# Seven block products in place of eight for a gelu MLP's second matrix product: block sums on GpSimd, partial sums in the output buffer

## The chip, the cores and the metric

The kernel runs on one core of one Trainium2 chip. The metric is device time in microseconds (us).

A profile is one execution. Its span is about 1.8 us shorter than the device time of the same run (323.7 against 325.46 us in the kernel before). Shares, waits and tile times below are of spans.

## The reference

A sliding-window attention, and then a two-layer MLP with gelu (tanh form) on its output.

```python
def _attn_ref(q, k, v):                      # 8 batches, 8 heads, 576 positions, 64 wide
    scores = scale * np.matmul(q, k.transpose(0, 1, 3, 2))
    scores = np.where(np.abs(pos[:, None] - pos[None, :]) <= 32, scores, -1e9)
    ...                                      # softmax
    return np.matmul(attn, v)

def _moe_ref(x, w_in, w_out):                # x 4608x512, w_in 512x2048, w_out 2048x512
    h = x @ w_in
    g = 0.5 * h * (1.0 + np.tanh(c * (h + 0.044715 * h * h * h)))
    return g @ w_out
```

The change touches only the last line, `g @ w_out`.

## The kernel before

The 4608 tokens are worked in nine tiles of 512. For each tile, the first product makes gT (2048 x 512, transposed, fp16) in 16 groups of four matmuls, each closed by a gelu on ScalarE. The second product makes the tile's output in four blocks of 128 tokens, each of 16 matmuls of 512 columns. Between those matmuls the attention of the next batch is strewn by a plan: `s` scores, `v` weighing of the values, `m` masks, `x` the spread of the result.

```python
    def ffn_in(t, fc, d0=0, d1=4):
        ...
        for dc in range(d0, d1):
            nc.tensor.matmul(ph, w_in16[:, dc, fc * 128:fc * 128 + 128],
                             xT[:, dc, t * 512 % RING:t * 512 % RING + 512],
                             start=(dc == 0), stop=(dc == 3))
        if d1 == 4:
            nc.scalar.activation(gTs[t][:, fc, :], ph, AF.Gelu_apprx_tanh)

    def ffn_out(t, t4, fc):
        ...                                  # the last block of the last tile in two halves of 256 columns
            nc.tensor.matmul(py[:, cols], gTs[t][:, f, t4 * 128:t4 * 128 + 128],
                             w_out16[:, f, cols], start=(f == 0), stop=(f == NF - 1))
        if f == NF - 1:
            yo = yp.tile([128, 512], FP32, name="yo", tag="yo")      # yp has 3 buffers
            ...                              # one copy out of PSUM, then the stores of the block
    ...
    for t in range(NT):
        ...
            if att and b > 1:
                cast_and_turn(b)             # VectorE casts of q and k, DMA transposes
            for fc in range(begun, NF):
                ffn_in(t, fc)
        ...
        for i in range(64):                  # second product, with attention of batch t+1 between
```

The softmax here doesn't subtract the row's maximum and nothing guards it: scores larger than these inputs give would overflow.

## Time and profile before

| | before |
|---|---|
| device time | 324.94 us, median of 3 (324.78 to 324.95) |
| span of the profiled run | 323.7 us |
| a steady tile (start of one first product to the next) | 33.6 us, TensorE busy for all of it |
| a tile without attention ahead (tile 7) | 28.3 us |
| from the start of the last matmul to the end | 3.9 us |

### The profile page before, as it was taken

The numbers are of one execution on the slowest core, as the hardware profiler recorded it, in microseconds if no ns is written. First come the engines' busy times: TensorE is split into PE (matmuls) and PEld (weight loads), VectorE is DVE, ScalarE is ACT, GpSimd is POOL, SyncE is SP. The second block draws the span as 40 slices with busy tenths as digits, with TensorE's granted clock in tenths as the row PEclk, the third lists the DMA queues.
The fourth block names the chain that finished last, engine by engine and source line by source line (L and its number), as shares of the span: only waits on it lengthen the run. The fifth ranks groups of instructions, "written<-read, shape, count | busy, mean of one in ns | idle before, by whom it ended". The sixth has DMA issues, their size and how long they took to land.

```text
span 323.7 us, 5827 instructions
## 1 busy us (share of the span) xinstructions
PE 311.7 (96%) x2265; PEld 153.4 (47%) x2265; DVE 136.0 (42%) x290; ACT 201.8 (62%) x316; POOL 59.5 (18%) x82
## 2 busy tenths in 40 slices
PE   7688999999999999999999999999999999999995
PEld 2463545444554445444544454445444544444444
DVE  5655587641556064705570467034713530110011
ACT  1757577578667766777577766777668577705600
POOL 3646356292031101300040104010000000000000
PEclk9959999999999999999999999999999999999999
DMA  7999998999989596949495979799270220031022
GB/s 208 259 362 362 381 277 230 251 161 157 248 155 160 95 245 159 169 88 251 115 155 116 221 161 135 134 203 183 75 122 17 67 58 9 0 91 41 0 60 70
DMA packets 120490, 50.57 MB, mean 156 GB/s; under 512 B 100784, under 2 KB 112048, under 8 KB 120464
## 3 DMA queue, kind: packets, MB, share of 16 engines
q1 hardware_dynamic: 88752, 45.07, 58.2%
q0 software_dynamic: 31520, 4.98, 21.0%
q8 instruction: 17, 0.28, 0.4%
q10 hardware_dynamic: 192, 0.16, 0.2%
q14 instruction: 9, 0.07, 0.1%
HBM read 37.62 MB, written 9.44 MB: 145 GB/s over the span
## 4 chain that ended last, share of the span: by engine, by line
PE 93%; SPq 2%; DMA 2%; DVE 1%; ACT 0%; issue 0%; POOL 0%; POOLq 0%
PE mm L461 39%; PE mm L439 24%; PE ph L439 14%; PE ps_o L381 5%; PE ps_s L348 5%; PE ps_d L381 4%; DMA vr<-in_v_dram 2%; SPq L126 1%; PE py L461 1%; ACT gT L443 0%; SPq L135 0%; PE pt L277 0%; DVE w_out L186 0%; PE pt L279 0%; DVE KT L285 0%
## 5 line engine op out<-in xcount | busy, mean ns | idle before, releaser
L461 PE MATMUL mm<-w_out,gT 128*128 128x512 f16 (+1 forms) x576 | 132.0, 377 | 0.8 <-DVE w_out L186 0.8
L439 PE MATMUL mm<-xT,w_in 128*128 128x512 f16 x360 | 89.0, 382 | 0.0
L439 PEld LDWEIGHTS <-w_in 128*128 128x128 f16 x576 | 56.2, 98 | 68.6 <-DVE w_in L186 1.5
L461 PEld LDWEIGHTS <-gT 128*128 128x128 f16 x592 | 54.2, 98 | 61.8 <-issue 0.6
L443 ACT ACTIVATE gT<-mm 128x512 f16<-128x512 f32 x90 | 53.7, 597 | 35.5 <-PE mm L439 35.5
L439 PE MATMUL ph<-xT,w_in 128*128 128x512 f16 x216 | 57.3, 381 | 1.2 <-ACT gT L443 1.2
L354 ACT ACTIVATE pe<-ps_s 128x704 f16<-128x704 f32 x64 | 43.3, 727 | 9.9 <-PE ps_s L348 9.2
L395 ACT ACTIVATE lt<-ps_d 128x480 f32<-128x480 f32 (+3 forms) x40 | 22.2, 555 | 43.2 <-PE ps_d L381 43.1
L443 ACT ACTIVATE gT<-ph 128x512 f16<-128x512 f32 x54 | 32.2, 597 | 13.3 <-PE ph L439 13.3
L405 DVE TENSOR_TENSOR xT<-ps_o,lt 128x480 f16<-128x480 f32 (+5 forms) x38 | 20.3, 552 | 46.9 <-ACT lt L396 46.8
L411 DVE TENSOR_TENSOR xT<-ps_o,lt 128x384 f16<-128x384 f32 (+1 forms) x8 | 4.3, 541 | 80.7 <-ACT lt L396 80.7
L363 DVE TENSOR_TENSOR pe<-pe,mask 128x704 f16<-128x704 f16 x64 | 34.4, 543 | 6.3 <-ACT pe L354 4.0
L465 DVE COPY yo<-mm 128x512 f32<-128x512 f32 x35 | 23.9, 685 | 31.1 <-PE mm L461 28.4
L166 POOL DMA_DIRECT2D V<-in_v_dram x24 | 23.8, 1005 | 63.6 <-PE ps_o L381 47.4
L381 PEld LDWEIGHTS <-V 128*64 128x64 f16 x336 | 18.9, 114 | 18.1 <-issue 11.9
L381 PE MATMUL ps_o<-pe,V 128*64 128x160 f16 (+2 forms) x244 | 22.8, 249 | 1.6 <-POOL V L258 1.5
L396 ACT ACTIVATE lt<-lt 128x480 f32<-128x480 f32 (+3 forms) x40 | 23.5, 588 | 1.3
L381 PE MATMUL ps_d<-pe,ones 128*64 128x192 f16 (+2 forms) x264 | 23.8, 246 | 0.0
L348 PE MATMUL ps_s<-QT,KT 64*128 64x192 f16 (+5 forms) x336 | 19.1, 230 | 2.2 <-DVE KT L285 2.2
L381 PEld LDWEIGHTS <-ones 128*64 128x64 f16 x336 | 19.5, 115 | 0.0
L348 PEld LDWEIGHTS <-KT 64*128 64x128 f16 x336 | 10.9, 95 | 10.6 <-issue 4.2
L168 POOL DMA_DIRECT2D V<-in_v_dram x6 | 5.3, 878 | 56.3 <-PE ps_d L381 39.2
(56 smaller groups left out, 154.3 us busy)
## 6 DMA issues: line engine op xcount, KB each, us to landing
kr<-in_k_dram SPq DMA_DIRECT2D x32, 256.0 KB
qr<-in_q_dram SPq DMA_DIRECT2D x6, 1024.0 KB
V<-in_v_dram POOLq DMA_DIRECT2D x30, 128.0 KB, 5.6
wst<-in_moe_w_in_dram SPq DMA_DIRECT2D x3, 1024.0 KB
wst<-in_moe_w_out_dram SPq DMA_DIRECT2D x3, 1024.0 KB
qr<-in_q_dram SPq DMA_DIRECT2D x8, 256.0 KB
vr<-in_v_dram SPq DMA_DIRECT2D x16, 128.0 KB
out_dram<-yo SPq DMA_DIRECT2D x30, 48.0 KB
```

The source lines that it names most:

```text
L166: nc.gpsimd.dma_start(V[:, c, :, :], v[b, :, 128 * c:128 * c + 128, :].rearrange("h p d -> p h d"))
L348: nc.tensor.matmul(ps[:, h, off:off + 4 * n].rearrange("k (j p) -> k j p", j=4), KTs[b % 2][r0:r0 + 64, pr, k0:k0 + 128], QTs[b][r0:r0 + 6 ...
L354: nc.scalar.activation(pe, ps[:, :, 0:w], AF.Exp, scale=SCALE)
L363: nc.vector.tensor_tensor(pe, pe, m.rearrange("p (o w) -> p o w", o=1).broadcast_to(list(pe.shape)), op=ALU.mult)
L381: nc.tensor.matmul(bk[r0:r0 + 64, at:at + 4 * n].rearrange("d (j p) -> d j p", j=4)[:, :, p0 - q0:p1 - q0], V[:, c, 2 * pr + h, :] if w == ...
L395: nc.scalar.activation(lt[:, 0:n], d[:, 0:n], AF.Ln)
L396: nc.scalar.activation(lt[:, 0:n], lt[:, 0:n], AF.Exp, scale=-1.0)
L405: nc.vector.tensor_tensor(xT[:, g, pos:pos + e], o[:, done:done + e], lt[:, done:done + e], op=ALU.mult)
L439: nc.tensor.matmul(ph, w_in16[:, dc, fc * 128:fc * 128 + 128], xT[:, dc, t * 512 % RING:t * 512 % RING + 512], start=(dc == 0), stop=(dc = ...
L443: nc.scalar.activation(gTs[t][:, fc, :], ph, AF.Gelu_apprx_tanh)
L461: nc.tensor.matmul(py[:, cols], gTs[t][:, f, t4 * 128:t4 * 128 + 128], w_out16[:, f, cols], start=(f == 0), stop=(f == NF - 1))
L465: (nc.scalar.copy if last and half == 0 else nc.vector.tensor_copy)(yo[:, cols], py[:, cols])
```

## The change

The intent: one level of a fast 2x2 block scheme for tiles 1 to 8. The tile's g (512 tokens x 2048) and w_out (2048 x 512) are cut into 2x2 blocks. Seven block products of 16 matmuls of 256 columns do the work of eight, so TensorE works an eighth less in the second product. The price is four sums of blocks of g for each tile (S1 to S4), four of blocks of w_out once (T1 to T4), and five extra additions on the outputs, done while PSUM (the memory in which TensorE sums) is copied out: the output buffer itself holds the partial sums M1, U2 and U3.

```diff
+WINO = [("A11", "B11", True), ("S2", "T2", True), ("A12", "B21", False), ("S3", "T3", False),
+        ("S1", "T1", True), ("A22", "T4", False), ("S4", "B22", False)]
+PLAN = {6: "s0 v-1", 24: "s1", 26: "m0", 32: "x-1", 40: "m1", 42: "v0 s2", ... }     # cut
-    yp = ctx.enter_context(tc.tile_pool(name="yp", bufs=3))
+    yp = ctx.enter_context(tc.tile_pool(name="yp", bufs=2))
@@ ffn_in
+        fc = n // 2 + 8 * (n % 2) if t else n
             nc.scalar.activation(gTs[t][:, fc, :], ph, AF.Gelu_apprx_tanh)
+            if t and n % 4 == 3:
+                sums(t, n // 4)
+    def combine_w():                                     # once, behind tile 0
+        for dst, x, y in ((T1, B12, B11), (T2, B22, T1), (T3, B22, B12), (T4, B21, T2)):
+            nc.gpsimd.tensor_tensor(dst, x, y, op=ALU.subtract)          # 128x2048 fp16
+    def sums(t, i):                                      # chunk i of 4, 128x512 fp16 each
+        eng = nc.vector if t == 1 else nc.gpsimd
+        for dst, x, y, op in ((S1, A21, A22, ALU.add), (S2, S1, A11, ALU.subtract),
+                              (S3, A11, A21, ALU.subtract), (S4, A12, S2, ALU.subtract)):
+            eng.tensor_tensor(dst, x, y, op=op)
@@ ffn_out, after each 16 matmuls
+        if n == 0:
+            nc.vector.tensor_copy(M1, py)
+        elif n == 1:
+            nc.vector.tensor_tensor(U2, py, M1, op=ALU.add)
+        ...                                              # C11, U3, C22, C21
+            for x in range(2):
+                store(t, 2 + x, yo[:, 2 + x, :])
+                if end:
+                    store(t, x, yo[:, x, :], left)
+    def ffn_last(t):                                     # C12 after the seventh product, in two halves
```

More of the change, by code (lines that the diff above doesn't have):

```diff
@@ L35, in width @@
     return sum(4 * (p1 - p0) for (_, _, p0, p1) in pieces)
-PLAN = {3: ([-1], [0]), 14: ([], [1]), 24: ([0], [2]), 35: ([1], [3]), 46: ([2], [4]), 58: ([3], [])}
+WINO = [("A11", "B11", True), ("S2", "T2", True), ("A12", "B21", False), ("S3", "T3", False),
+        ("S1", "T1", True), ("A22", "T4", False), ("S4", "B22", False)]
+PLAN = {6: "s0 v-1", 24: "s1", 26: "m0", 32: "x-1", 40: "m1", 42: "v0 s2", 48: "x0", 56: "m2",
+        61: "v1 s3", 64: "x1", 80: "m3", 81: "v2 s4", 88: "x2", 101: "v3", 104: "m4", 112: "x3"}
 TURN_0 = {9: 0, 11: 1, 13: 2, 15: 3}
@@ L49 @@
            [(t4, fc) for t4 in (2, 3) for fc in range(16)])
-END = (3, 0, 2, 1)
 RING = 1536
@@ L413, in spread, with ffn_in @@
                 lt[:, 0:n].rearrange("d (r q) -> d r q", r=NPAIR), op=ALU.mult)
-    def values(b, g):
-        o, d = weigh(b, g)
-        spread(b, g, o, invert(b, g, d))
     gTs = {}
     phs = {}
-    def ffn_in(t, fc, d0=0, d1=4):
-        if fc == 0 and d0 == 0:
+    def ffn_in(t, n, d0=0, d1=4):
+        fc = n // 2 + 8 * (n % 2) if t else n
+        if n == 0 and d0 == 0:
             gTs[t] = gp.tile([128, NF, 512], FP16, name="gT", tag="gT")
@@ L432, in ffn_in @@
                 if t:
-                    i = (0, 2, 1)[fc % 3] if fc < NF - 1 else 2
+                    i = (first(t), 2, 1 - first(t))[n % 3] if n < NF - 1 else 2
                 else:
@@ L443, in ffn_in, with first @@
             nc.scalar.activation(gTs[t][:, fc, :], ph, AF.Gelu_apprx_tanh)
+            if t and n % 4 == 3:
+                sums(t, n // 4)
+    def first(t):
+        return (t + 1) % 2
+    wino = {}
+    def combine_w():
+        t12 = stage.tile([128, 2, 8, 256], FP16, name="t12", tag="stage")
+        t34 = stage.tile([128, 2, 8, 256], FP16, name="t34", tag="stage")
+        B11, B12, B21, B22 = (w_out16[:, r:r + 8, c:c + 256] for r in (0, 8) for c in (0, 256))
+        T1, T2, T3, T4 = t12[:, 0], t12[:, 1], t34[:, 0], t34[:, 1]
+        for dst, x, y in ((T1, B12, B11), (T2, B22, T1), (T3, B22, B12), (T4, B21, T2)):
+            nc.gpsimd.tensor_tensor(dst, x, y, op=ALU.subtract)
+        s12 = stage.tile([128, 2, 8, 256], FP16, name="s12", tag="stage")
+        s34 = stage.tile([128, 2, 8, 256], FP16, name="s34", tag="stage")
+        yo = stage.tile([128, 4, 512], FP32, name="y4", tag="stage")
+        wino.update(B11=B11, B21=B21, B22=B22, T1=T1, T2=T2, T3=T3, T4=T4, S1=s12[:, 0],
+                    S2=s12[:, 1], S3=s34[:, 0], S4=s34[:, 1], yo=yo)
@@ new lines, in sums @@
+    def sums(t, i):
+        g, r = gTs[t], slice(2 * i, 2 * i + 2)
+        A11, A21, A12, A22 = (g[:, r0 + 2 * i:r0 + 2 * i + 2, c:c + 256]
+                              for r0 in (0, 8) for c in (0, 256))
+        S1, S2, S3, S4 = (wino[f"S{n}"][:, r, :] for n in (1, 2, 3, 4))
+        eng = nc.vector if t == 1 else nc.gpsimd
+        for dst, x, y, op in ((S1, A21, A22, ALU.add), (S2, S1, A11, ALU.subtract),
+                              (S3, A11, A21, ALU.subtract), (S4, A12, S2, ALU.subtract)):
+            eng.tensor_tensor(dst, x, y, op=op)
@@ L445 @@
     out_v = out.rearrange("(b p j) f -> b j p f", b=B, j=4)
     pys = {}
-    def ffn_out(t, t4, fc):
-        last = t == NT - 1 and t4 == END[-1]
-        if last:
-            half, fc = divmod(2 * fc, NF)
-            halves = [slice(256 * half, 256 * half + 256)] * 2
-        else:
-            half, halves = 0, [slice(0, 512)]
-        for f, cols in enumerate(halves, fc):
-            if f == 0:
-                pys[t4] = bank((END.index(t4) if t == NT - 1 else t4) % 2) if half == 0 else \
-                    psO.tile([128, 512], FP32, name="py2", tag="O")
-            py = pys[t4]
-            nc.tensor.matmul(py[:, cols], gTs[t][:, f, t4 * 128:t4 * 128 + 128],
-                             w_out16[:, f, cols], start=(f == 0), stop=(f == NF - 1))
-        if f == NF - 1:
-            yo = yp.tile([128, 512], FP32, name="yo", tag="yo")
-            (nc.scalar.copy if last and half == 0 else nc.vector.tensor_copy)(
-                yo[:, cols], py[:, cols])
-            m = 0
-            while m < 128:
-                b, c = divmod(t * 512 + t4 * 128 + m, S)
-                q0, n = (0, cut(b)) if c < 4 * cut(b) else (cut(b), 144 - cut(b))
-                j, p = divmod(c - 4 * q0, n)
-                e = min(n - p, 128 - m)
-                eng = nc.scalar if last and m else nc.sync if t else nc.gpsimd
-                eng.dma_start(out_v[b, j, q0 + p:q0 + p + e, cols], yo[m:m + e, cols])
-                m += e
@@ new lines, in store, with ffn_out_0 @@
+    def store(t, t4, yo, cols=slice(0, 512), eng=None):
+        m = 0
+        while m < 128:
+            b, c = divmod(t * 512 + t4 * 128 + m, S)
+            q0, n = (0, cut(b)) if c < 4 * cut(b) else (cut(b), 144 - cut(b))
+            j, p = divmod(c - 4 * q0, n)
+            e = min(n - p, 128 - m)
+            (eng or nc.sync).dma_start(out_v[b, j, q0 + p:q0 + p + e, cols], yo[m:m + e, cols])
+            m += e
+    def ffn_out_0(t4, fc):
+        if fc == 0:
+            pys[t4] = bank(t4 % 2)
+        nc.tensor.matmul(pys[t4], gTs[0][:, fc, t4 * 128:t4 * 128 + 128], w_out16[:, fc, :],
+                         start=(fc == 0), stop=(fc == NF - 1))
+        if fc == NF - 1:
+            yo = yp.tile([128, 512], FP32, name="yo", tag="yo")
+            nc.vector.tensor_copy(yo, pys[t4])
+            store(0, t4, yo, eng=nc.gpsimd)
@@ new lines, in ffn_out @@
+    def ffn_out(t, i):
+        n, blk, f = i // 16, i // 8 % 2, i % 8
+        a, w, new = WINO[n]
+        if i % 16 == 0 and new:
+            pys[n % 2] = bank((first(t) + n) % 2)
+        py = pys[n % 2].rearrange("p (b c) -> p b c", b=2)
+        if a[0] == "A":
+            r0, c0 = 8 * (int(a[2]) - 1) + f, 256 * (int(a[1]) - 1) + 128 * blk
+            lhsT = gTs[t][:, r0, c0:c0 + 128]
+        else:
+            lhsT = wino[a][:, f, 128 * blk:128 * blk + 128]
+        nc.tensor.matmul(py[:, blk, :], lhsT, wino[w][:, f, :], start=(new and i % 16 == 0),
+                         stop=(i % 16 == 15), skip_group_check=True)
+        if i % 16 < 15:
+            return
+        yo, left, right = wino["yo"], slice(0, 256), slice(256, 512)
+        C11, C12, C21, C22 = (yo[:, r:r + 2, c] for r in (0, 2) for c in (left, right))
+        end = t == NT - 1
+        M1, U2, U3 = C21, C12, C22
+        if n == 0:
+            nc.vector.tensor_copy(M1, py)
+        elif n == 1:
+            nc.vector.tensor_tensor(U2, py, M1, op=ALU.add)
+        elif n == 2:
+            nc.vector.tensor_copy(C11, py)
+        elif n == 3:
+            nc.vector.tensor_tensor(U3, py, M1, op=ALU.add)
+        elif n == 4:
+            nc.vector.tensor_tensor(C22, py, U3, op=ALU.add)
+        elif n == 5:
+            nc.vector.tensor_tensor(C21, py, M1, op=ALU.add)
+            for x in range(2):
+                store(t, 2 + x, yo[:, 2 + x, :])
+                if end:
+                    store(t, x, yo[:, x, :], left)
@@ L478 @@
+    def ffn_last(t):
+        py = pys[0].rearrange("p (b c) -> p b c", b=2)
+        yo, right = wino["yo"], slice(256, 512)
+        for x in range(2):
+            nc.vector.tensor_tensor(yo[:, x, right], py[:, x, :], yo[:, x, right], op=ALU.add)
+            store(t, x, yo[:, x, :], right if t == NT - 1 else slice(0, 512))
     cast_open(0)
@@ L588 @@
                 ffn_in(t, fc)
-        plan = PLAN if att else {3: ([-1], [])} if t == B - 1 else {}
+        plan = PLAN_0 if not t else PLAN if att else {6: "v-1", 32: "x-1"} if t == B - 1 else {}
         def group(g):
@@ L597 @@
             load_qk(b + 1)
-        if t == 0:
-            ods = {}
-        for i in range(64):
-            for act in PLAN_0.get(i, "").split() if t == 0 else ():
+        ods = {}
+        for i in range(113 if t else 65):
+            for act in plan.get(i, "").split():
                 kind, g = act[0], int(act[1:])
@@ L623 @@
                     ods[g] = (o, invert(bb, gg, d))
+                    if t and g < 0 and b + 1 < B:
+                        load_v(b + 1)
                 else:
                     spread(*group(g), *ods[g])
-            if t and i in plan:
-                for g in plan[i][0]:
-                    values(*group(g))
-                    if g < 0 and b + 1 < B:
-                        load_v(b + 1)
-                for g in plan[i][1]:
-                    score(*group(g))
-                    mask(*group(g))
-            if t:
-                ffn_out(t, END[i // NF] if t == NT - 1 else i // NF, i % NF)
-            else:
-                ffn_out(t, *ORDER_0[i])
+            if t == 0 and i < 64:
+                ffn_out_0(*ORDER_0[i])
+            elif t and i < 112:
+                ffn_out(t, i)
         if t == 0:
             load_v(2)
+            combine_w()
+        else:
+            ffn_last(t)
         begun = 2 if att else 0
```

## The prediction

> **What bounds the kernel now.** I read the page first: busy shares, then the chain that ended last, then the costliest groups.
>
> ```profile
> PE 311.7 (96%) x2265; PEld 153.4 (47%) x2265; DVE 136.0 (42%) x290; ACT 201.8 (62%) x316; POOL 59.5 (18%) x82
> ...
> PE 93%; SPq 2%; DMA 2%; DVE 1%; ACT 0%; issue 0%; POOL 0%; POOLq 0%
> ...
> L461 PE MATMUL mm<-w_out,gT 128*128 128x512 f16 (+1 forms) x576 | 132.0, 377 | 0.8 <-DVE w_out L186 0.8
> ```
>
> TensorE is the bound: 93% of the chain is its own, and the second product (L461) waited 0.8 us in the whole run. Busy 377 ns per matmul is not its cost, for matmuls overlap; cost is start-to-start spacing. The timeline of TensorE in the last tile gives that at two widths:
>
> ```profile
> 306.09 12.27 PE L461 MATMUL mm<-w_out,gT 128*128 128x512 f16 x64
> 318.19 1.91 PE L461 MATMUL py<-w_out,gT 128*128 128x256 f16 x16
> ```
>
> 306.09 to 318.19 holds 48 matmuls of 512 columns and 16 of 256 columns: 48 x 0.216 + 16 x 0.108 = 12.1 us. So a 256-column matmul with a fresh 128x128 weight load already runs at half the price of a 512 one. Sums by stretch over two steady tiles (first product, then second product with attention):
>
> ```profile
> 129.59:143.40 13.81, 13.81 (x65) 6.27 (x64) 6.16 (x15) 10.14 (x17) 2.64 (x3) 1.00 1.08 139
> 143.40:163.19 19.79, 19.79 (x185) 9.96 (x184) 8.93 (x16) 13.35 (x21) 2.32 (x3) 1.00 0.79 168
> ```
>
> TensorE (second number after the stretch) is busy for all of it, at full clock, in a 33.6 us period. Any TensorE time saved is time saved, unless a new wait takes its place. GpSimd (the number before the clock) has 2 to 3 us of work per stretch: room in total; latency is the question.
>
> **What the Trainium skill says.** (1) "TensorE: Matmul & The Clock Gate", Back-to-back issue gap: a warm matmul costs about N/2.4 + 2.5 ns, 216 ns at 512 columns; the trace agrees at 512 (0.216), and at 256 shows 0.108. (2) "GPSIMD Engine Reference", 3.1 Elementwise: a two-input elementwise operation takes about 2.5 cycles per element because both inputs share one read port; 2048 fp32 columns took 4.5 us. No two-input GpSimd operation is in this trace. One-input casts of 128x512 are, in uncontended pairs of 1.18 us:
>
> ```profile
> 23.98 1.18 POOL L186 CAST w_in<-wst 128x512 f16<-128x512 f32 x2 [1.48 <-DMA wst<-in_moe_w_in_dram]
> 26.69 1.62 POOL L186 CAST w_in<-wst 128x512 f16<-128x512 f32 x2 [1.53 <-DMA wst<-in_moe_w_in_dram]
> ```
>
> (3) "SBUF — State Buffer", Who interferes with whom: VectorE in a two-port mode, or with two SBUF inputs, and GpSimd reading SBUF block each other. The second line agrees: beside two VectorE casts the same pair took 1.62.
>
> **The change part by part.**
> Removed: per tile 1 to 8, 64 matmuls x 0.216 = 13.82 us. Added: 7 products x 16 matmuls x 0.108 = 12.10 us. Gain 1.73 us a tile, 13.8 us in eight: 311 us if nothing waits.
>
> Added on GpSimd (tiles 2 to 8): four chunks of four sums, 128x512 fp16, two inputs. Estimate from the skill's GPSIMD page: a quarter of 4.5 us, 1.12 us each, 18 us a tile. Half-width types might be faster, but the trace speaks against it: the fp16 fills of 192 and 128 columns took 259 and 205 ns, 0.84 ns a column, one column a cycle, so not packed. In a tile, counted from the start of its first product at 129.59: gelu 3 (133.24 + 0.60) opens chunk 1 at 4.25; gelu 15 (143.60 + 0.60) opens chunk 4 at 14.61. A chunk opens every 3.46 us but takes 4 x 1.12 = 4.5, so GpSimd falls behind. S2 of chunk 4 is its 14th operation: 4.25 + 14 x 1.12 = 19.9. TensorE wants it in the second block product, at its seventh matmul: 13.81 + 22 x 0.108 + 0.40 (score 0, 144.67 to 145.07) + 0.53 (tail weighing, 144.14 to 144.67) = 17.1. That is a stall of 2.8 us a tile, more than the gain. About eight VectorE casts of 0.35 us still run when chunk 1 opens and share the port: I add 0.5. So 3.3 x 7 = 23 us. Break-even is 12 operations fitting between 4.25 and about 15.3: some 0.92 us each.
>
> Added once: four weight combinations of 128x2048 on GpSimd, 4.5 us each, from the end of the V load (69.83 + 0.88 = 70.7) to 88.7. Tile 1 has its block sums on VectorE meanwhile, two SBUF inputs against the same port. Tile 1's second product starts at 76.2 and wants sums from about 79; if VectorE gets one operation between two long GpSimd ones, the stall is near 10 us, if they interleave finely, near 0. I take 5.
>
> Moved on VectorE: four copies of 0.69 us become six full and two half evictions, 6 x 0.69 + 2 x 0.43 = 5.0 us in place of 2.8 a tile, beside TensorE. Each bank now comes back after one product of 1.7 us, with 0.7 us of eviction in it: thin but enough. One ordering wait shows: the weighing of pair 0 needs the tail's spread, which stands behind an eviction: about 0.4 us x 6 = 2, hidden where the tile already stalled on GpSimd.
>
> End: two half evictions of 0.43 and more stores through one queue: +1 us.
>
> Sum of this, the likeliest branch: 324.9 - 13.8 + 23 + 5 + 1 = 340 us.
>
> **The rivals.** (A) GpSimd is fast enough, 0.9 us or less. Then only the small terms stay: 324.9 - 13.8 + 2 + 2 (tile 1) + 1 = 316 us. For it: the chunk cadence of 3.46 us and one early S2 look designed to fit, and whoever moved tile 1 alone to VectorE did not find the others in need. Against it: the cast and fill durations above. (B) The port conflict is what hurts: masks and casts on VectorE and sums on GpSimd hold each other up for whole operations, K transposes start late, and stalls grow to 4 or 5 us a tile with perhaps a lowered clock after each: 345 to 355. For it: 1.18 against 1.62 above. Against: VectorE is nearly idle from 135.8 to 146.6 of a steady tile, where most sums fall. (C) The output's single buffer makes the first copy of a tile wait for stores. Against: stores of a tile are issued at least 14 us ahead of it; near 0.
>
> **Range and chances.** The outcome has two humps, 316 and 340, decided by one duration that the trace does not hold. I give rival A 0.38, the stalling branches 0.48, and 0.14 to something between, where stall and gain cancel. The predicted time, 330 us, is the middle of these chances rather than one of the humps; 312 to 352 takes in both.
>
> **What would show it.** A two-input GpSimd operation of 128x512 at 1.1 us, and "POOL s" as releaser of L514's idle time of some 20 us, confirm the main branch; 0.9 or less, or idle under 5 us, refute it. Tile 1 waiting on VectorE sums during the four long subtractions confirms the 5 us term. Spacing of the new matmuls must be 0.108; if it is more, weight loads are the bound and the 13.8 is wrong. The number fails most likely through the GpSimd duration, next through tile 1.

## More of the kernel before

The page's map of the run in 40 slices shows the state that the change starts from. Each digit is a share in tenths: of a slice's time in which TensorE was busy, and of full speed for its granted clock (the first digits are the start-up).

```profile
PE   7688999999999999999999999999999999999995
...
PEclk9959999999999999999999999999999999999999
```

TensorE never stops after the start-up, and its clock is never lowered.

## The result, and the profile after

| | before | after |
|---|---|---|
| device time, median of 4 | 324.86 us | 381.79 us (378.61 to 382.47) |
| ratio | | 1.1747, 95% interval 1.1681 to 1.1813 |
| span of the profiled run | 323.7 us | 376.9 us |
| granted clock, mean of the span | 0.984 | 0.929 |

A ratio here and below is the mean time of one kernel's fast runs over the mean of the other's of the same rounds, so it is not quite the ratio of the medians (the changed kernel's holds a fifth run, of 383.18 us). The change is slower by 17%, where the prediction had given 312 to 352 us.

The page of the changed kernel, with the lines that answer to those of before: busy shares, the two rows of slices, the chain (the work that ended last, followed back from the end), and the two groups that matter.

```profile
PE 316.1 (84%) x2633; PEld 195.3 (52%) x2633; DVE 178.7 (47%) x338; ACT 200.5 (53%) x315; POOL 206.2 (55%) x198
...
PE   7689997943999499869988798959896989699591
...
PEclk9879999995899989996999899989996999899988
...
PE 45%; POOL 25%; issue 9%; DMA 8%; SPq 7%; ACT 3%; DVE 1%; POOLq 0%; DVEq 0%; ACTq 0%
...
L477 POOL TENSOR_TENSOR s<-gT 128x512 f16<-128x512 f16 x56 | 68.2, 1218 | 117.7 <-ACT gT L444 117.7
...
L514 PE MATMUL mm<-t,s 128*128 128x256 f16 x384 | 56.3, 300 | 38.3 <-POOL s L477 27.4
```

TensorE's row now has a dip in every tile, and the row of its clock has one behind each. GpSimd carries a quarter of the chain. Its sums of two blocks of g, 128x512, take 1.22 us on average, near the 1.12 us estimated. TensorE's busy time went up (311.7 to 316.1), though it has an eighth less to do in the second product: that is the lowered clock.

Who held TensorE up, from the table of waits (engine, line, releaser: us in total, times, longest):

```profile
PE mm L514 <- POOL s L477: 27.4, 8, 4.7
PE mm L514 <- DVE s L477: 10.9, 4, 8.8
PE mm L440 <- ACT gT L444: 5.0, 6, 0.9
```

**One steady tile.** The timeline of TensorE in tile 2 (start, us, what, count, idle before it):

```profile
126.77 0.39 PE L514 MATMUL mm<-t,s 128*128 128x256 f16 x2 [0.16 <-POOL s L477]
131.85 0.49 PE L514 MATMUL mm<-t,s 128*128 128x256 f16 x2 [4.69 <-POOL s L477]
132.27 0.74 PE L351 MATMUL ps_s<-QT,KT 64*128 64x160 f16 x8
132.94 1.89 PE L514 MATMUL mm<-t,s 128*128 128x256 f16 x8
```

The seventh matmul of the second block product waited 4.69 us for S2 of chunk 4. The eight matmuls behind it begin at 132.94 and the next product at 134.62: 1.68 / 8 = 0.21 us apiece, double the 0.108 of a 256-column matmul at full clock. The Trainium skill, "TensorE: Matmul & The Clock Gate", Part 1, says that TensorE's clock falls to half after some 3.4 us of idleness and returns after as long of work. This trace agrees on the fall: after each of the seven long waits of tiles 2 to 8 (3.44 to 4.69 us) the granted clock reads 0.50, and the mean of these tiles is 0.91 to 0.96. It came back 2.6 to 6.1 us after TensorE had started again, so the time of the return agrees only roughly.

GpSimd in the same tile:

```profile
113.81 2.55 POOL L477 TENSOR_TENSOR s<-gT 128x512 f16<-128x512 f16 x1 [21.35 <-ACT gT L444]
116.44 1.15 POOL L477 TENSOR_TENSOR s<-s,gT 128x512 f16<-128x512 f16 x1
117.55 1.15 POOL L477 TENSOR_TENSOR s<-gT 128x512 f16<-128x512 f16 x1
...
129.17 1.39 POOL L477 TENSOR_TENSOR s<-gT 128x512 f16<-128x512 f16 x1
130.64 1.15 POOL L477 TENSOR_TENSOR s<-s,gT 128x512 f16<-128x512 f16 x1
```

Independent sums start 1.11 us apart. The first took 2.55 us, beside a run of VectorE casts (113.60 to 115.35). The 14th, S2 of chunk 4, started at 130.64. GpSimd never paused in between: it was late because its queue was long.

**Tile 1.** VectorE had the block sums there, and GpSimd the four weight combinations. Both engines over the same stretch:

```profile
75.82 4.17 DVE L477 TENSOR_TENSOR s<-s,gT 128x512 f16<-128x512 f16 x1
79.92 4.27 DVE L477 TENSOR_TENSOR s<-gT 128x512 f16<-128x512 f16 x1
84.11 4.26 DVE L477 TENSOR_TENSOR s<-gT,s 128x512 f16<-128x512 f16 x1
88.29 0.41 DVE L477 TENSOR_TENSOR s<-gT 128x512 f16<-128x512 f16 x1
```

```profile
79.68 4.23 POOL L461 TENSOR_TENSOR t<-w_out 128x2048 f16<-128x2048 f16 x1
83.86 4.22 POOL L461 TENSOR_TENSOR t<-w_out,t 128x2048 f16<-128x2048 f16 x1
```

A 0.41 us sum took 4.2 us while a GpSimd subtraction of 4.2 us ran; when the last of these ended, at 88.08, the same sums took 0.41 us again. One small operation got in between two large ones, as the prediction feared. TensorE stood still for 8.8 us at a stretch.

The casts ahead of these sums were held up too:

```profile
65.17 8.61 DVE L308 CAST qt<-qt 16x512 f16<-16x512 f32 x4
```

The same four took 2.11 us in the kernel before. One of them lasted from 66.93 to 73.77, the end of the first GpSimd subtraction (69.39 to 73.48), though it began while GpSimd was still issuing loads. So VectorE's first sum began only at 75.38.

**The account.** Tile times are from the start of one first product to the next; busy time is TensorE's in each tile.

| part of the 53.2 us between the spans | us |
|---|---|
| seven products in place of eight, 8 x 1.73 | -13.8 |
| TensorE waiting for GpSimd's sums, tiles 2 to 8 | +27.4 |
| TensorE waiting for VectorE's sums, tile 1 | +10.9 |
| lowered clock: busy time beyond that of the same tiles at clock 1.00, all eight tiles | +18.6 |
| first product waiting for a late gelu, tiles 3 to 8 | +5.0 |
| longer tail after the last matmul (7.8 against 3.9) | +3.9 |
| later start of tile 1, a wait for a spread | +0.9 |
| sum | +52.9 |

For the fourth row, the busy time of a tile at full clock is that of a later run (`sums_dve`: 31.9 us in tiles 2 to 6, 26.7 in tile 7, 25.9 in tile 8; for tile 1 I took 31.9). Tile 1 alone lost 3.7, tiles 2 to 8 lost 14.9.

### The profile page after: what moved, and what is told of

Its sections match the earlier page's. It is cut to its first block, busy times and chain, and to the rows that moved or that the text cites. A ratio compares the mean times of both kernels' runs of the same rounds, so it can differ in the third digit from the quotient of the medians.

```text
span 376.9 us, 6730 instructions
## 1 busy us (share of the span) xinstructions
PE 316.1 (84%) x2633; PEld 195.3 (52%) x2633; DVE 178.7 (47%) x338; ACT 200.5 (53%) x315; POOL 206.2 (55%) x198
## 4 chain that ended last, share of the span: by engine, by line
PE 45%; POOL 25%; issue 9%; DMA 8%; SPq 7%; ACT 3%; DVE 1%; POOLq 0%; DVEq 0%; ACTq 0%
PE mm L514 23%; POOL s L477 19%; PE mm L440 10%; PE ph L440 6%; POOL t L461 4%; SPq L138 4%; DMA wst<-in_moe_w_in_dram 3%; PE ps_s L351 3%; PE ps_o L384 2%; DMA qr<-in_q_dram 2%; ACT L444 2%; PE ps_d L384 2%; POOL V L169 1%; DMA out_dram<-yo 1%; ACT gT L444 1%
## 5 line engine op out<-in xcount | busy, mean ns | idle before, releaser
L477 POOL TENSOR_TENSOR s<-gT 128x512 f16<-128x512 f16 x56 | 68.2, 1218 | 117.7 <-ACT gT L444 117.7
L514 PE MATMUL mm<-t,s 128*128 128x256 f16 x384 | 56.3, 300 | 38.3 <-POOL s L477 27.4
L514 PEld LDWEIGHTS <-s 128*128 128x128 f16 x512 | 50.3, 103 | 52.2 <-POOL s L477 29.7
L524 DVE COPY y<-mm 128x512 f32<-128x512 f32 x8 | 5.5, 691 | 90.2 <-PE mm L514 90.2
L514 PEld LDWEIGHTS <-gT 128*128 128x128 f16 x384 | 39.5, 107 | 10.7
L366 DVE TENSOR_TENSOR pe<-pe,mask 128x704 f16<-128x704 f16 x64 | 40.1, 661 | 1.8 <-ACT pe L357 1.6
L514 PE MATMUL mm<-w_out,gT 128*128 128x256 f16 x256 | 39.0, 306 | 0.0
L477 POOL TENSOR_TENSOR s<-s,gT 128x512 f16<-128x512 f16 x28 | 32.8, 1170 | 2.2
L477 POOL TENSOR_TENSOR s<-gT,s 128x512 f16<-128x512 f16 x28 | 32.5, 1162 | 0.0
```

Of the source, the lines that this page charges most:

```text
L366: nc.vector.tensor_tensor(pe, pe, m.rearrange("p (o w) -> p o w", o=1).broadcast_to(list(pe.shape)), op=ALU.mult)
L477: eng.tensor_tensor(dst, x, y, op=op)
L514: nc.tensor.matmul(py[:, blk, :], lhsT, wino[w][:, f, :], start=(new and i % 16 == 0), stop=(i % 16 == 15), skip_group_check=True)
```

## The experiments

Theories at the start. **Lateness:** GpSimd's queue is too long for the moment at which S2 is wanted, and the rest (clock, gelu) follows from that. **Port:** VectorE and GpSimd block each other at the port to SBUF (the on-chip buffer) that they share, and that is the cost. **Narrow products:** 256-column matmuls cost more than half.

### s12first: only GpSimd's order changes

```diff
             if t and n % 4 == 3:
-                sums(t, n // 4)
+                sums(t, n // 4, (1, 2, 3, 4) if t == 1 else (1, 2))
+            if t > 1 and n == NF - 1:
+                for which in (3, 4):
+                    for i in range(4):
+                        sums(t, i, (which,))
```

> All block sums stay on GpSimd in tiles 2 to 8; only their order changes: S1 and S2 of each chunk first, all S3 and then all S4 after the last chunk. Theory 1 (lateness: S2 of chunk 4 is GpSimd's 14th operation at 1.11 us each): S2 of chunk 4 becomes the 8th and is ready about 2.3 us after the last gelu, so the 3.8 to 4.7 us stall of tiles 2 to 8 at the seventh matmul of the second product falls under 0.5 us, the granted clock after it returns to 1.0 and a tile takes about 33.6 - 1.7 + 0.9 (late gelu table) = 32.8 us; the time falls by 35 to 45 us from 381, to 336 to 346. Theory 2 (the shared SBUF port is what hurts): GpSimd and VectorE do the same work beside each other, so most of the loss stays and the time is above 365. Theory 3 (256-column products cost more than half): above 365 too, with no idle to show for it.

Measured: 350.76 us (348.64 to 352.84), ratio to before 1.0822 (1.0769 to 1.0876). GpSimd does the same 112 sums; TensorE's wait for them fell from 27.4 us to 2.2. Tiles 2 and 3 by the view of stretches (span, TensorE busy, weight loads, VectorE, ScalarE, GpSimd, clock, DMA):

```profile
110.03:143.10 33.07, 31.95 (x299) 20.78 (x297) 19.84 (x36) 23.38 (x38) 25.57 (x21) 1.00 0.89 148
143.10:177.26 34.16, 32.10 (x299) 20.82 (x297) 19.75 (x35) 23.28 (x38) 24.44 (x21) 1.00 0.97 155
```

Lateness was 31 us of the loss, and the clock is 1.00 again. Busy time of 31.95 us against 33.6 before is the 1.7 us a tile that the block products were to give: narrow products are out. But I had expected 336 to 346, and the rest has a name: waits for a spread on VectorE (7.3 us in all) that I had put at nothing, beside the gelu (5.0). The port is a second, smaller cost. Measured below.

### spin: dummy matmuls into the wait

```diff
+                if t > 1 and i == 22:
+                    ps = psO.tile([128, 512], FP32, name="spin", tag="D")
+                    for _ in range(14):
+                        nc.tensor.matmul(ps, w_in16[:, 0, 0:128], w_in16[:, 0, 0:512],
+                                         start=True, stop=True)
```

> The changed kernel plus 14 dummy 512-column matmuls in tiles 2 to 8 just ahead of the matmul that waits for GpSimd, result unused, so that TensorE is busy for 3.0 of the some 4 us of waiting. If the lowered clock after the stall comes from TensorE's idleness, granted clock goes from 0.93 to about 0.96 (tile 1 still stalls), the waits for GpSimd shrink by what the dummies fill, and the time falls by 7 x 1.9 to 3.1 us, some 13 to 20 us, to 361 to 368. If the clock is lowered for another reason (power, narrow matmuls), the time stays at 378 to 384.

Measured: 368.60 us (367.37 to 369.62), ratio to before 1.1348 (1.1309 to 1.1388): 13 us faster than the change while doing more work. Tiles 2 and 3 in the view of stretches, the changed kernel first:

```profile
109.48:148.05 38.57, 33.72 (x298) 21.43 (x296) 17.75 (x36) 23.48 (x38) 24.25 (x21) 0.96 1.12 139
148.05:187.71 39.66, 34.95 (x298) 22.20 (x296) 17.65 (x35) 23.38 (x38) 23.00 (x21) 0.91 0.97 132
```

```profile
112.40:149.65 37.25, 35.40 (x313) 22.14 (x310) 17.77 (x36) 23.49 (x38) 24.28 (x21) 1.00 1.00 143
149.65:186.71 37.06, 35.39 (x313) 22.21 (x310) 17.64 (x35) 23.39 (x38) 23.00 (x21) 1.00 0.97 142
```

The clock, the last number but two, is 1.00 with waits for GpSimd of at most 1.5 us. So idleness lowered it, not power or the width of the matmuls. The dummies win 1.3 to 2.6 us in each of tiles 2 to 8, 11.9 in all; the account above charges the clock there with 14.9, and the runs do not settle the 3 us between.

### gelu_table: where the table load waits

Ahead of each tile's first gelu ScalarE loads the table of the gelu, implicitly. In the kernel before, the load waits for nothing and the gelu for TensorE:

```profile
129.62 1.28 ACT L443 ACT_TABLE_LOAD   x1
131.30 0.60 ACT L443 ACTIVATE gT<-mm 128x512 f16<-128x512 f32 x1 [0.40 <-PE mm L439]
```

In tile 3 of the changed kernel it is the load that waits for TensorE, so a load that could have run early begins when the matmuls end:

```profile
149.81 1.28 ACT L444 ACT_TABLE_LOAD   x1 [1.65 <-PE mm L440]
151.10 0.60 ACT L444 ACTIVATE gT<-mm 128x512 f16<-128x512 f32 x1
```

I put this down to the gelu's second wait: GpSimd reads the old gT, so the first gelu must wait for GpSimd as well as for TensorE, and one of the two waits goes to the load ahead of it. The traces do not show which wait an instruction carries, but they fit: in tile 2, ahead of which GpSimd made no sums, the load (at 109.60) does not wait, nor does it in tile 3 of `sums_dve` (141.89).

The experiment loads the table explicitly, behind the last attention activation.

```diff
+        if t and t < B:
+            load_gelu_table()
         for fc in range(begun):
             ffn_in(t + 1, fc, 0, 3)
```

> The changed kernel with an explicit load of the gelu table right behind the last attention activation of a tile, in place of the implicit one, which in tiles 3 to 8 carries a wait on TensorE because the first gelu now has two waits. Theory: the 0.94 us idle of TensorE at the fourth chunk of the first product (tiles 3 to 7) and 0.3 in tile 8 go, 5.0 us in all; but the last gelu is not earlier by as much as GpSimd's chunk 1 is, so the GpSimd sums start 0.9 earlier too and the stall behind them stays the same: time down by 4 to 6 us to 375 to 378. Rival: the stall behind GpSimd is the floor and eats the gain: within 1 us of 381.

Measured: 379.74 us (379.56 to 380.20), ratio 1.1695 (1.1667 to 1.1724). The trace is clear: TensorE's 5.0 us of waiting for that gelu is gone. Its wait for GpSimd rose from 27.4 to 31.3 us. The gain was eaten by the next wait, as the rival had it; the 2 us that the time fell by are within the scatter of the changed kernel (378.6 to 383.2).

### comb_dve: the weight combinations on VectorE

```diff
-            nc.gpsimd.tensor_tensor(dst, x, y, op=ALU.subtract)
+            nc.vector.tensor_tensor(dst, x, y, op=ALU.subtract)
@@ called behind cast_and_turn of tile 1 in place of behind tile 0
```

> The four 128x2048 weight combinations move from GpSimd to VectorE, behind the casts of tile 1. Theory 1 and 2 agree on this part: the tile-1 stall of about 11 us (VectorE's sums stood 4.2 us each behind a GpSimd subtraction of 4.1 us) falls to 0 to 3 us, VectorE needs about 1.2 us for each combination, and the time falls by 9 to 13 us to 368 to 372. Tiles 2 to 8 do not change. If VectorE's sums are slow by themselves, tile 1 keeps more than 6 us.

Measured: 367.31 us (364.65 to 368.91), ratio 1.1302 (1.1246 to 1.1359). Tile 1 fell from 46.5 to 32.9 us, and no wait for VectorE's sums is left. The gain is 14 us, a little more than the 9 to 13 expected, since the clock of tile 1 came back too (0.85 to 0.98), which I had not counted.

### sums_dve: one word

```diff
-        eng = nc.vector if t == 1 else nc.gpsimd
+        eng = nc.vector
```

> One word of the changed kernel changes: the block sums of every tile run on VectorE (0.42 us each in the trace of the changed kernel, against 1.15 on GpSimd); the weight combinations stay on GpSimd. Lateness theory: S2 of chunk 4 follows the last gelu by under 1 us, so the GpSimd stall, the lowered clock and the late gelu table (the first gelu waits for GpSimd only because GpSimd read the activations) all go in tiles 2 to 8: about 32.0 us for a tile with attention; tile 1 keeps its 46.5 us. Time about 381 - 5 x 6.9 - 2 x 6 = 331 to 336. Rival: VectorE, with 5.5 us of casts and 6.7 us of sums inside 13.8 us of first product, becomes the new wait, by late K transposes or late evictions: tiles stay above 34 us and the time above 342.

Measured: 333.44 us (332.50 to 334.38), ratio 1.0270 (1.0232 to 1.0308). Tiles 1, 2 and 3:

```profile
63.81:109.65 45.84, 34.95 (x297) 21.41 (x296) 39.77 (x52) 22.80 (x37) 29.58 (x17) 0.85 0.91 122
109.65:141.77 32.12, 31.87 (x298) 20.84 (x296) 22.29 (x52) 23.38 (x38) 4.17 (x6) 1.00 1.04 166
141.77:173.89 32.12, 31.87 (x298) 20.82 (x296) 22.33 (x51) 23.39 (x38) 4.95 (x6) 1.00 0.99 164
```

Waits for GpSimd's sums, late gelu and lowered clock vanish together from tiles 2 to 8, and VectorE, with 22.3 us of work in 32.1, is no new bound. What remains over before is tile 1.

### best_dve and best_pool: everything mended, with the sums on either engine

`best_dve` joins sums_dve, comb_dve, gelu_table and the last stores on ScalarE's queue; `best_pool` joins s12first with the latter three.

> Everything that the traces charge, mended at once: block sums and weight combinations on VectorE, explicit gelu table, last stores on ScalarE's queue. Theory: tile 1 about 32.9 us, tiles 2 to 6 about 32.0, tiles 7 and 8 about 26.6 and 25.8, tail 5.5 in place of 7.8: span about 315, time 313 to 318, ratio to before 0.965 to 0.98, so the block products are worth their 1.7 us a tile. If 256-column products or the seven evictions cost something that the stalls hid, the ratio is above 0.985.

> The sums of tiles 2 to 8 stay on GpSimd, S1 and S2 first; weight combinations on VectorE, explicit gelu table, last stores on ScalarE's queue. Theory: what is left of the loss is the port: in the run with S1 and S2 first the weighing of pair 0 waited up to 1.1 us for a spread that stands behind masks held up by GpSimd. Tile 1 about 32.9, tiles 2 to 6 about 32.5 to 34.2, time 318 to 327, so 1 to 3% behind the version with all on VectorE. If it equals that version within 1%, the port costs nothing here.

Measured: best_dve 320.37 us (318.39 to 321.51), ratio 0.9849 (0.9812 to 0.9885); best_pool 330.22 us (329.40 to 331.99), ratio 1.0169 (1.0130 to 1.0207). Both came out a few us above what I had expected. The tiles were as foreseen (32.1 us for best_dve, 33.1 mostly for best_pool); the start and the tail were not, see below.

The two kernels, which differ in where the sums run and in their order, lie 3% apart, and the port shows in best_pool's VectorE and GpSimd at the same time in tile 3:

```profile
149.79 2.59 DVE L373 TENSOR_TENSOR pe<-pe,mask 128x704 f16<-128x704 f16 x2
...
153.37 1.87 DVE L373 TENSOR_TENSOR pe<-pe,mask 128x704 f16<-128x704 f16 x2
```

```profile
149.49 5.40 POOL L490 TENSOR_TENSOR s<-gT 128x512 f16<-128x512 f16 x4
154.85 5.28 POOL L490 TENSOR_TENSOR s<-gT,s 128x512 f16<-128x512 f16 x4
```

Two masks, 0.92 us where GpSimd makes no sums (in the changed kernel at 135.94), took 1.9 to 2.6; four sums took 5.3 to 5.4 in place of 4 x 1.11. The spread behind the masks then came late: TensorE waited for spreads 6.6 us in the run, against 1.5 in best_dve, and 2.2 us for sums of GpSimd. Tiles 2 to 8 are 1.3 us longer each, 8.8 in all; 5.1 of it, some 0.7 us a tile, is the longer waiting for spreads that stand behind held-up masks: that much the port costs here.

### tail: the last stores on a second queue

```diff
-            store(t, x, yo[:, x, :], right if t == NT - 1 else slice(0, 512))
+            store(t, x, yo[:, x, :], right if t == NT - 1 else slice(0, 512),
+                  nc.scalar if t == NT - 1 else None)
```

> The changed kernel with the stores of the last two half evictions on ScalarE's queue. In the changed kernel 15 stores left one queue from 368.35 on in 6.1 us and the run ended 7.8 us after the last matmul began, against 3.9 before. Theory: the queue is the bound of the tail, which falls to about 5.5 us. Rival: the transfers themselves bound it, tail within 0.5 us of 7.8.

One look: 381.25 us, state unknown. The end came 7.5 us after the start of the last matmul, against 7.84. My expectation failed. The four moved stores left ScalarE's queue in 1.94 us, but the eleven others still needed 5.86 us of the first queue, because all are issued after the sixth product.

### before_yp2, best_yp3, best3: the third output buffer, and stores as blocks are finished

In every variant so far tile 1 began later (63 to 66 us) than in the kernel before (62.4). The change also takes an output buffer from tile 0; its third copy there then waits for the first store to land. The changed kernel's timelines of VectorE and of TensorE's weight loads:

```profile
59.89 0.69 DVE L499 COPY yo<-mm 128x512 f32<-128x512 f32 x1 [3.91 <-DMA out_dram<-yo]
...
60.83 0.09 PEld L351 LDWEIGHTS <-KT 64*128 64x128 f16 x1 [2.48 <-DVE KT L273]
```

before_yp2 is the kernel before with `bufs=2` in place of `bufs=3`; best_yp3 is best_dve with `bufs=3`; best3 is that, and in the last tile stores C11 after the third product, C22 after the fifth, the left half of C21 after the sixth.

> The kernel before with one number changed: two output buffers in place of three, as the change has it. Theory: the third eviction of tile 0 waits for the first store to land (3.9 us on VectorE in the changed kernel), the last score of tile 0 stands behind it (2.3 us on TensorE), and in the later tiles four evictions share two buffers too: at least 2 us more, 326.5 to 329. Rival: the later start of tile 1 in the variants (63 to 66 us against 62.4) is scatter of the input transfers: within 1 us of before.

> The version with all sums on VectorE (320.4 us) with three output buffers for tile 0 again. Theory: tile 1 starts at 62 to 62.7 us in place of 64.4 and the time falls by 1.5 to 2.5 us, to 318 to 319. Rival, scatter of the inputs: within 0.7 us of 320.4.

> As the run with three output buffers, and the last tile's blocks leave as they are finished: C11 after the third product, C22 after the fifth, the left half of C21 after the sixth, the right half of the first rows last. Theory: the tail falls from 7.4 us after the last matmul to 4.0 to 5.0, because the 11 stores that left one queue in 5.7 us are spread; 2 to 3 us faster than the run with three buffers alone, 315 to 317, ratio to before 0.965 to 0.977.

Measured in the same rounds: before_yp2 328.71 us (326.80 to 330.56), ratio 1.0118 (1.0084 to 1.0153). best_yp3 317.45 us (316.81 to 318.77), ratio 0.9781 (0.9759 to 0.9803). best3 315.83 us (314.45 to 317.27), ratio 0.9724 (0.9700 to 0.9749). The lost buffer costs 1.2% by itself; the rival, scatter of the input transfers, is refuted as the whole of it. The early stores gave 1.6 us and a tail of 5.7 us, less than I had expected: the profile, which was of the slowest of six runs, still shows 12 stores taking 5.2 us of one queue.

best3 beats both kernels. Its page:

```profile
PE 298.3 (95%) x2633; PEld 188.8 (60%) x2633; DVE 200.8 (64%) x454; ACT 200.9 (64%) x315; POOL 59.6 (19%) x82
...
PEclk9959999999999999999999999999999999999999
```

TensorE is the bound again, at full clock, with 298.3 us of work in place of 311.7: 13.4 of the 13.8 us.

## Why the prediction was wrong

It named slower as likeliest (0.48) and the stall at S2 of chunk 4 as the cause, and both held. The number, 330, was the middle between two branches. Even the likeliest branch alone, 340 us, falls short, and the range ended at 352. The step that failed most is the cost of a stall: the sum charged the idle time alone, and the lowered clock behind it cost 18.6 us more.

- **The gain.** 1.73 us a tile, 256-column matmuls at 0.108 us: right. Tiles at full clock have 31.9 us of TensorE work.
- **GpSimd's duration.** Estimated 1.12 us, measured 1.11 apart: right, so rival A (0.9 us or less) is false. (The prediction's 2.5 cycles per element are about 2.6 in the section that it names.) Its argument from the look of the code ("designed to fit") was worth nothing against two rows of the trace.
- **The stall of tiles 2 to 8.** The term 3.3 x 7 = 23 us measured 27.4. TensorE asked nearly when predicted (17.1 us into the tile; 17.7 in tile 2), but S2 came at 22.3 in place of 20.4: 1.4 us for the first sum behind casts, 0.5 behind masks, and 0.12 for each of the four sums that wait on the one just before. The 0.5 us for the port was too small.
- **Tile 1.** The term of 5 us measured 10.9. I had named 10 as what one small operation between two large ones would cost and took the middle; the trace has just that pattern.
- **The clock.** The main sum has no term for it, and rival B only a "perhaps". B's stalls of 4 or 5 us nearly came (3.4 to 4.7), from a long queue and not from the port alone, yet its 355 is still 27 us short of the 381.79. The lowered clock measured 18.6 us, a third of the whole. I had worked out a stall of about 3 us and did not ask what happens to TensorE's clock near 3.4. The spin run shows that idleness is the cause.
- **The gelu.** Absent from the prediction: 5.0 us of waiting, from a wait that moved onto a table load. Its removal alone gained nothing clear, since TensorE waited for GpSimd just as long.
- **The end.** The term of 1 us measured 3.9. I counted evictions, and not that up to 15 stores then wait for one queue.
- **VectorE's ordering wait.** The 2 us measured 0.3 in the changed kernel, since the stalls hide it, and 1.6 in best3.
- **The output buffer.** Absent, though "bufs=2" stands in the diff. In the changed kernel it hides in a start later by 0.6 us; alone it costs 1.2%.
- **Rival C,** the single buffer of later tiles making the first copy wait for stores: no such wait among the listed ones of TensorE or VectorE. Right to set at zero.

With the measured terms the sum is 324.9 - 13.8 + 27.4 + 10.9 + 18.6 + 5.0 + 3.9 + 0.9 = 377.8 us; the profiled run took 378.61.

What stays open: how much of best_pool's 1.3 us a tile is masks held up and how much is the longer sums of GpSimd; and why before_yp2 lost 3.9 us while the changed kernel's tile 1 began only 0.6 later (starts in the variants with two buffers range from 63.0 to 65.8 us).

## What to carry to other kernels

Work moved off the bounding engine must arrive in time: give each result the moment at which it is wanted and the place of its operation in the helper's queue, and order the queue by need. A wait of the matrix engine is paid for a second time when it is long enough to lower the clock: here waits of 3.4 us and more were, and in the steady tiles of the spin run waits of 1.5 us and less were not. Put two-input sums on VectorE rather than GpSimd while VectorE has room, and never set a long GpSimd operation beside short VectorE ones that need the shared port.

## What the Trainium skill lacked or had wrong

- "GPSIMD Engine Reference", 3.1 Elementwise: it gives one two-input duration, 4.5 us for 2048 fp32 columns. Here fp16 is hardly faster: 4.1 to 4.2 us for 2048 columns, 1.11 us apart for 512, and 0.12 us more where a sum reads the one before.
- "SBUF — State Buffer", Who interferes with whom: that one engine blocks the other for a whole operation agrees (0.41 us became 4.2). It does not say that a run of short VectorE operations keeps the port: the first sum of tile 2 took 2.55 us beside five casts.
- "TensorE: Matmul & The Clock Gate", Back-to-back issue gap: its figure of 131 ns for a stream of weight loads and 512-column matmuls is not seen; here such a stream runs at 216 ns, and at 108 ns for 256 columns. The page's formula N/2.4 + 2.5, which it gives for a matmul by itself, fits (216 and 109).
- None of the pages read has it that an implicit activation table load can wait for the input of the activation behind it (here when GpSimd had read the activation's output buffer): it cost 0.94 us in each of tiles 3 to 7.
